# A fused attention, mixer and gated-feed-forward kernel: one weight slice loaded earlier, spreads placed behind given tiles, and four products moved from GpSimd to VectorE

## The chip, the cores and the metric

The kernel runs on one core of a Trainium2 chip. The metric is the device time of one execution in microseconds (us). The engines are PE (TensorE: matmuls, accumulating in PSUM), DVE (VectorE), ACT (ScalarE), POOL (GpSimd) and SP (SyncE, which issues every DMA here). Each engine works through its own instructions in a fixed order and waits on semaphores for the others.

## The reference

Three parts follow one another, in float32 (q, k, v of 2 x 12 x 448 x 64; the token axis is 448, the model axis 768):

```python
# 1 causal attention
scores = where(mask, -1e9, q @ k.T / sqrt(64)); attn = softmax(scores); x = attn @ v     # x: [2, 448, 768]
# 2 mixer: tokens, then channels
u = x + (relu(x.T @ w_tok1) @ w_tok2).T                  # 448 -> 256 -> 448
x = u + relu(u @ w_ch1) @ w_ch2                          # 768 -> 1536 -> 768
# 3 gated feed-forward
h = gelu_tanh(x @ w_in); u, v = h[..., :512], h[..., 512:]
v_n = (v - mean(v)) / sqrt(var(v) + 1e-6) * g_ln
gated = u * (w_sg @ v_n + b_sg[:, None])                 # w_sg mixes the 448 tokens
out = x + gated @ w_out                                  # 512 -> 768
```

The weights are given in float64 and are unpacked on the chip.

## The kernel before, in words

**Numbers.** Matmuls with full precision are made of three f16 (or fp32r) matmuls: a value is split into a high and a low part, and high by high, high by low and low by high are added in PSUM (`mm3`, lines 174 to 181; its three matmuls are L178, L179 and L180 in every trace row). Before an f16 split a tensor is scaled by its largest absolute value. That maximum is found per partition on an engine and then carried over all partitions by `spread` (lines 156 to 161): one small PE matmul of 128x128 (L158) into a PSUM bank, then three small DVE operations (L159 maximum, L160, L161 reciprocal). The split is ACT (high part) and DVE (low part) in `split16` (L165, L166), or ACT, ACT and POOL in `split16p` (L170, L171, L172).

**Weights.** `decode` (lines 104 to 124) loads a float64 slice by DMA into one of two `wraw` buffers, and makes float32 of it with one ACT operation (L120) and two DVE operations (L123, L124). `load_w2` (lines 546 to 555) decodes one of the six slices of w_ch2, in two halves, into buffers `w2m`, of which there are four, and takes the sum of absolute values of each half on ACT (L553) and their maximum on DVE (L151, the column `w2am0` to `w2am5`). `end_w2` (lines 557 to 569) spreads that column and splits the slice. `begin16` and `end16` (lines 599 to 606 and 664 to 672) do the same for the slices of w_in and w_out; w_out has six slices, 4 to 9 of the counter j.

**Stages.** First attention with the token mixing (to about 165 us). Then r: `channel_up`, twelve tiles of 36 matmuls for each of the two batches, u by w_ch1. Then y: `channel_down`, twelve tiles of 36 matmuls, r by w_ch2, written y(m,b) below for slice m and batch b. The loop of lines 608 to 624 makes y(0,0); y(1,0), y(0,1); y(2,0), y(1,1); and so on, and in each round calls `end_w2(m + 2)` and `load_w2(m + 3)`. Each y tile is taken from PSUM by DVE (L233, `yt`), completed by POOL (L235) and its maximum taken by DVE (L146, `yam`). r of batch 1 is split in `split_r(1)` while y(1,0) runs: twelve ACT operations (L165) and twelve on DVE (L166). Then v (`v_ps`) and u (`ug_ps`) of the gated part with the normalisation, then the mixing over tokens (lines 747 to 765): four tiles g of 11 matmuls for each batch (`g_ps`). DVE scales a g tile and adds b_sg (L761, `gt`), POOL multiplies it into the array `ug` (L763; batch 1 in two pieces, since its tokens lie rotated by 64), and DVE takes the maximum (L146, `gtam`). Once the four tiles of a batch are done, their maximum (L151, `gtam16_0`, `gtam16_1`) is spread, and the products are split (`gate16`, `gt_hi` and `gt_lo`). Last come twelve output tiles o of 12 matmuls, and the writing of the result.

**Order.** A scheduler with a timeline simulation of its own sets the order of each engine's instructions when the program is built; the order in which the code is written and the construct `tc.issue_after(x)` (not before instruction x) only guide it. So PE can stand at a spread whose column is late while matmuls that are ready are queued behind it.

Of the kernel before, what the change touches and what calls it, by code (L numbers as in the profile page):

```python
# [28 lines left out]
def mixer_kernel(  # L29
# [18 lines left out]
    nc = tc.nc  # L48
    B, H2, D2, S = q.shape
# [6 lines left out]
    NCC = C // P  # L56
# [117 lines left out]
    def mm3(ps, pairs, begun=False):  # L174

        n, done = len(pairs), []
        for i, ((lh, ll), (rh, rl)) in enumerate(pairs):
            nc.tensor.matmul(ps, lh, rh, start=i == 0 and not begun, stop=False)  # L178
            nc.tensor.matmul(ps, lh, rl, start=False, stop=False)  # L179
            done.append(nc.tensor.matmul(ps, ll, rh, start=False, stop=i == n - 1).ins)  # L180
        return done
# [345 lines left out]
    with rs:  # L527
        ps_d = ctx.enter_context(tc.tile_pool(name="ps_d", bufs=8, space=PSUM, reuse_waits="tile"))
        r1pool = rs.enter_context(tc.tile_pool(name="r1pool", bufs=1, reuse_waits="tile"))
        tmp = rs.enter_context(tc.tile_pool(name="tmp", bufs=3, reuse_waits="tile"))  # L530
        def pst(name):
            return ps_d.tile([P, 512], F32, tag="d", name=name)

        def split_r(b):

            am = top_of(rsum[:, b], f"ram{b}")
            spread(pst("rs_ps"), am, *rsc[b], TOP)
            for c in range(NFF):
                if b == 0:
                    t = r1pool.tile([P, 2, S], F16, name=f"r16_{c}")  # L540
                else:
                    t = (rpool if c < NF0 else r1pool).tile([P, 2, S], F16, tag=f"r{c}_0", name=f"r16_{c}")
                split16(t[:, 0], t[:, 1], r_of[c, b], rsc[b][1][:, 0:1])
                r_of[c, b] = t

        def load_w2(m):

            ms = []
            for i in range(2):
                w = tmp.tile([P, WC], F32, tag="w2m", name="w2m", bufs=4)  # L550
                decode(w, w_ch2[m, :, i * NCC:(i + 1) * NCC, :].rearrange("p a f -> p (a f)"))
                unused = tmp.tile([P, WC], BF16, tag="w2a", name="w2a", bufs=1)
                nc.scalar.activation(unused, w, AF.Abs, accum_out=w2sum[:, m, i:i + 1])  # L553
                ms.append(w)
            w2_begun[m] = ms, top_of(w2sum[:, m], f"w2am{m}")

        def end_w2(m):

            ms, am = w2_begun.pop(m)
            done = spread(pst("w2_ps"), am, *w2sc[m], TOP)  # L560
            ws[m] = []
            for i, w in enumerate(ms):
                if m < 2:
                    t = tmp.tile([P, 2, NCC, P], F16, name=f"w2_{m}{i}", bufs=1)
                else:
                    t = wpool.tile([P, 2, NCC, P], F16, tag=("whi", "wlo")[i], name="w2", bufs=3)
                split16p(*(t[:, h].rearrange("p a f -> p (a f)") for h in range(2)), w, w2sc[m][1][:, 0:1])
                ws[m] += [(t[:, 0, c, :], t[:, 1, c, :]) for c in range(NCC)]
            return done

        w2_begun, ws, w16, begun = {}, {}, {}, []
        tail = 4
        for m in [*range(NF0 - tail), *range(NF0, NFF), *range(NF0 - tail, NF0)]:
            channel_up(m, [1] if m < NF0 else [0, 1], r1pool, ps_d)
            if m == NF0 + 1:
                with tc.issue_after(last_load[0]):
                    load_w2(0)
            if m == NFF - 2:
                end_w2(0)
                load_w2(1)  # L580
            if m == NF0 - tail:
                end_w2(1)
                split_r(0)
            if m == NF0 - 1:
                load_w2(2)

        def to16(b):

            spread(pst("ys_ps"), yam16[b], *ysc[b], TOP)
            nc.vector.tensor_mul(vinv[:, 2 * b:2 * b + 1], ysc[b][0], wvsc[0])  # L590
            hs = slice(64 * b, 64 * b + 64)
            nc.vector.tensor_copy(vinv[hs, 1:2], vinv[hs, 2 * b:2 * b + 1])
            for m in range(NCC):
                y16[m][b] = upool.tile([P, 2, S], F16, tag=f"ul{m}_{b}", name=f"y16_{m}_{b}")
                split16(y16[m][b][:, 0], y16[m][b][:, 1], y32[m][b], ysc[b][1][:, 0:1])
                ts = slice((1 - b) * (S - 64), (1 - b) * (S - 64) + 64)
                nc.vector.tensor_copy(y3[:, :, m, 64 * b:64 * b + 64], y16[m][b][:, :, ts])

        def begin16(src, j):

            k = src.shape[1]
            m = wpool.tile([P, WC], F32, tag="wm", name="wm", bufs=3)[:, :k * P]
            decode(m, src.rearrange("p a f -> p (a f)"))
            am = wams[:, j:j + 1]
            absmax(am, m)
            begun.append((j, k, m, am))

        for m in range(NCC):
            channel_down(m, ws[m], [0], ps_d, tmp)
            if m == 0:  # L610
                with tc.issue_after(mms[0, 0][NFF // 2]):
                    split_r(1)
            if 0 < m < NCC - 1:
                channel_down(m - 1, ws[m - 1], [1], ps_d, tmp)
            if m + 2 < NCC:
                spread_last = end_w2(m + 2)
            with tc.issue_after(spread_last):
                if m + 3 < NCC:
                    load_w2(m + 3)
                for c in ([m], [m], [m], [m], [m, m + 1], [])[m]:  # L620
                    decode(wv32[:, c, :], w_inv[:, c, :])
                    absmax(wvam[:, c:c + 1], wv32[:, c, :])
                if m == NCC - 2:
                    wvam16 = top_of(wvam, "wvam16")
        spread(pst("wv_ps"), wvam16, *wvsc, TOP)
        for c in range(NCC):
            split16(wvh[:, c, :], wvl[:, c, :], wv32[:, c, :], wvsc[1][:, 0:1])
        with tc.issue_after(spread_last):
            for m in range(3):
                begin16(w_inu[m], m)  # L630
        channel_down(NCC - 2, ws[NCC - 2], [1], ps_d, tmp)
        to16(0)
        channel_down(NCC - 1, ws[NCC - 1], [1], ps_d, tmp)
        last_y = last_top[0]
# [8 lines left out]
    z_hi = gp.tile([P, NV, DH], F16, name="z_hi")  # L643
    z_lo = gp.tile([P, NV, DH], F16, name="z_lo")
# [19 lines left out]
    def end16():  # L664

        j, k, m, am = begun.pop(0)
        split = split16 if j < NDC else split16p
        spread(pst("w_ps"), am, winv[:, j:j + 1], wsc[:, j:j + 1], TOP)
        hi = gp.tile([P, k, P], F16, name=f"wh{j}")
        lo = gp.tile([P, k, P], F16, name=f"wl{j}")  # L670
        split(hi.rearrange("p a f -> p (a f)"), lo.rearrange("p a f -> p (a f)"), m, wsc[:, j:j + 1])
        w16[j] = hi, lo
# [66 lines left out]
    def gate16(b):  # L739

        us = slice(b * S, (b + 1) * S)
        spread(pst("gt_ps"), gtam16[b], *gtsc[b], TOP)
        nc.vector.tensor_scalar(oinv[:, b], winv[:, NDC:], gtsc[b][0][:, 0:1], None, ALU.mult)
        for m in range(NDC):
            split16(gt_hi[:, m, us], gt_lo[:, m, us], ug[:, m, us], gtsc[b][1][:, 0:1])

    for b in range(B):
        us = slice(b * S, (b + 1) * S)
        for m in range(NDC):
            if b == 0 and m < 2:  # L750
                end16()
            if b == 1 and m == 2:
                gate16(0)
            ds_ = slice(m * P, (m + 1) * P)
            pg = pst("g_ps")
            nc.tensor.matmul(pg[:, :S], zz[b][:, ds_], sgh[:, 3, :], start=True, stop=False)
            nc.tensor.matmul(pg[:, :S], zz[b][:, ds_], sgl[:, 3, :], start=False, stop=False)
            vts_ = [c + 4 * b for c in range(3)]
            mm3(pg[:, :S], [((z_hi[:, vt, ds_], z_lo[:, vt, ds_]), (sgh[:, c, :], sgl[:, c, :])) for c, vt in enumerate(vts_)], True)
            gt = gw.tile([P, S], F32, tag="gt", name="gt")  # L760
            nc.vector.scalar_tensor_tensor(gt, pg[:, :S], gcol[:, m:m + 1], bb, ALU.mult, ALU.add)  # L761
            for cs, ts in rotated(b):
                nc.gpsimd.tensor_mul(ug[:, m, cs], gt[:, ts], ug[:, m, cs])  # L763
            absmax(gtam[:, b, m:m + 1], ug[:, m, us])
        gtam16[b] = top_of(gtam[:, b], f"gtam16_{b}")
    last_gt = last_top[0]
# [65 lines left out]
```

## Time and profile before

| | |
|---|---|
| time, median of 3 runs | 422.99 us (421.78 to 426.54) |
| the profiled execution | 422.21 us |
| its span, first to last instruction | 420.1 us |
| PE busy | 389.7 us (93%) |
| DVE, ACT, POOL busy | 281.4, 248.5, 207.2 us |
| mean granted clock of PE | 0.994 |

The profiled execution lies between the fastest run and the median; 2.1 us of it lie outside the span. Busy time of PE is made of records whose ends are modelled, so the spacing of matmul starts says more: in y, g and o it is 0.19 us per matmul of 448 columns when nothing is missing. A granted clock of 1.00 is the higher of the two levels of PE (2.4 GHz), 0.50 the lower (1.2 GHz).

### The profile page before, as it was taken

How to read it: one execution, taken by the hardware profiler on the slowest of the kernel's cores; microseconds unless marked ns; L12 is line 12 of the kernel's file. 1: busy time of each engine (PE TensorE's matmuls, PEld its weight loads, DVE VectorE, ACT ScalarE, POOL GpSimd, SP SyncE). 2: the span in 40 equal slices, each digit the busy share in tenths (PEclk: the TensorE clock that was granted, in tenths of full speed). 3: DMA queues.
4: the chain of work that ended last, by engine and by line, in shares of the span. 5: the costliest groups of instructions: out<-in, count | busy, mean ns of one | idle time of the engine just before them, and what ended most of it. 6: DMA issues, size and time to landing. Idle time of an engine off the chain costs nothing.

```text
span 420.1 us, 7291 instructions
## 1 busy us (share of the span) xinstructions
PE 389.7 (93%) x2610; PEld 264.0 (63%) x2610; DVE 281.4 (67%) x689; ACT 248.5 (59%) x481; POOL 207.2 (49%) x211
## 2 busy tenths in 40 slices
PE   5868898796898999999999979999999999999996
PEld 3546777674787999999887534555554445544553
DVE  5979775799935635434356698666896896648832
ACT  3989776589775555754679676543256475562200
POOL 2786847679777573431452255344212666138200
PEclk9999999999999999999999998999999999999999
DMA  7999898999955844765540034436603032100122
GB/s 214 207 283 249 189 143 181 242 290 301 199 139 128 181 145 153 222 230 191 184 135 17 17 110 137 158 131 201 222 0 89 0 101 100 52 1 0 67 109 87
DMA packets 61459, 60.99 MB, mean 145 GB/s; under 512 B 47856, under 2 KB 53104, under 8 KB 61424
## 3 DMA queue, kind: packets, MB, share of 16 engines
q1 hardware_dynamic: 61424, 60.54, 53.3%
q8 instruction: 20, 0.33, 0.3%
q14 instruction: 15, 0.12, 0.1%
HBM read 46.50 MB, written 2.75 MB: 117 GB/s over the span
## 4 chain that ended last, share of the span: by engine, by line
PE 47%; DVE 13%; DMA 12%; POOL 11%; issue 8%; ACT 6%; SPq 2%; POOLq 0%; ACTq 0%; DVEq 0%
PE r_ps L179 6%; PE r_ps L180 6%; PE r_ps L178 6%; PE y_ps L178 5%; PE y_ps L180 5%; PE y_ps L179 5%; DMA vr<-in 5%; DMA pT<-hl 5%; POOL hl L357 3%; PE o_ps L179 2%; PE o_ps L180 2%; PE o_ps L178 2%; DMA wraw<-in 2%; DVE wm L124 2%; POOL wl L172 2%
## 5 line engine op out<-in xcount | busy, mean ns | idle before, releaser
L357 POOL TENSOR_TENSOR hl<-pe,hl 128x512 f16<-128x512 f32 x43 | 54.0, 1264 | 24.3 <-ACT hl L356 23.8
L330 PE MATMUL s_ps<-k,q 128*128 128x64 f32 (+3 forms) x216 | 54.7, 393 | 11.5 <-DVE mx L335 4.8
L100 POOL TENSOR_TENSOR wlo<-wm,whi 128x768 fp32r<-128x768 f32 x19 | 37.6, 1977 | 42.1 <-ACT whi L133 42.0
L178 PE MATMUL r_ps<-uh,whi 128*128 128x448 f32 x144 | 53.6, 372 | 0.0
L179 PE MATMUL r_ps<-ul,whi 128*128 128x448 f32 x144 | 53.3, 370 | 0.0
L180 PE MATMUL r_ps<-uh,wlo 128*128 128x448 f32 x144 | 53.0, 368 | 0.0
L120 ACT ACTIVATE wm<-wraw 128x768 f32<-128x768 f32 (+2 forms) x35 | 28.0, 800 | 41.7 <-DMA wraw<-in 25.9
L178 PE MATMUL y_ps<-r,w 128*128 128x448 f16 x144 | 51.4, 357 | 0.0
L179 PE MATMUL y_ps<-r,w 128*128 128x448 f16 x144 | 51.2, 356 | 0.0
L180 PE MATMUL y_ps<-r,w 128*128 128x448 f16 x144 | 51.2, 356 | 0.0
L123 DVE TENSOR_SCALAR wm<-wm 128x768 int32<-128x768 int32 (+2 forms) x35 | 21.7, 621 | 42.5 <-ACT wm L120 42.5
L330 PEld LDWEIGHTS s_ps<-k,q 128*128 128x128 f32 x216 | 30.2, 198 | 21.7 <-DVE mx L335 5.7
L235 POOL TENSOR_TENSOR y<-yt,ul 128x448 f32<-128x448 f32 x12 | 15.5, 1290 | 48.4 <-DVE yt L233 45.5
L335 DVE CUSTOM_DVE_ANT_0 pe<-s_ps,mask 128x192 f32<-128x192 f32 (+3 forms) x84 | 34.9, 443 | 5.4 <-PE s_ps L330 5.4
L124 DVE SCALAR_TENSOR_TENSOR wm<-wraw,wm 128x768 int32<-128x768 int32 (+2 forms) x35 | 35.4, 1013 | 0.6
L344 ACT ACTIVATE pe<-pe,bias 128x448 f32<-128x448 f32 (+3 forms) x74 | 35.3, 525 | 0.3
L381 PE MATMUL x_ps<-vh,pT 128*128 128x65 f16 (+1 forms) x240 | 25.9, 197 | 6.6 <-DMA pT<-hl 5.9
L356 ACT CAST hl<-pe 128x512 f16<-128x512 f32 x43 | 26.1, 610 | 9.2 <-DMA pT<-hl 8.9
L381 PEld LDWEIGHTS <-pT 128*128 128x128 f16 (+1 forms) x240 | 21.1, 98 | 13.4 <-DMA pT<-hl 8.7
L172 POOL TENSOR_TENSOR w<-w2m,w 128x768 f16<-128x768 f32 x12 | 21.3, 1791 | 15.3 <-ACT w L171 12.6
L179 PEld LDWEIGHTS r_ps<-ul,whi 128*128 128x128 f32 x144 | 27.0, 188 | 2.8 <-issue 0.4
L180 PEld LDWEIGHTS r_ps<-uh,wlo 128*128 128x128 f32 x144 | 27.0, 188 | 2.7 <-issue 0.2
(205 smaller groups left out, 1016.1 us busy)
## 6 DMA issues: line engine op xcount, KB each, us to landing
wraw<-in SPq DMA_DIRECT2D x35, 768.0 KB, 4.3
wraw<-in SPq DMA_DIRECT2D x14, 512.0 KB, 3.7
vr<-in SPq DMA_DIRECT2D x12, 320.0 KB, 3.7
k<-in SPq DMA_DIRECT2D x12, 224.0 KB, 3.1
q<-in SPq DMA_DIRECT2D x24, 112.0 KB, 3.6
out<-ob SPq DMA_DIRECT2D x12, 224.0 KB, 1.9
wraw<-in SPq DMA_DIRECT2D x3, 256.0 KB, 3.1
pT<-hl SPq DMA_TRANSPOSE x43, 4.1
```

The source lines that it names most:

```text
L100: nc.gpsimd.tensor_sub(lo, src, f32(hi))
L120: nc.scalar.activation(m, words.bitcast(F32)[:, :, 1], AF.Prelu, scale=2.0 ** -112, alpha=-(2.0 ** 32))
L124: nc.vector.scalar_tensor_tensor(mi, words[:, :, 0], 29, mi, ALU.logical_shift_right, ALU.bitwise_or)
L172: nc.gpsimd.tensor_sub(lo, m, hi)
L178: nc.tensor.matmul(ps, lh, rh, start=i == 0 and not begun, stop=False)
L179: nc.tensor.matmul(ps, lh, rl, start=False, stop=False)
L180: done.append(nc.tensor.matmul(ps, ll, rh, start=False, stop=i == n - 1).ins)
L330: nc.tensor.matmul(ps[:, o:o + m], qp[:, q0:q0 + P], k2[:, ks], start=True, stop=True)
L335: nc.vector.tensor_tensor_reduce(out=pe[:, cs], in0=ps[:, cs], in1=mask0 if i == 0 else mask[:, MASKS[i]], scale=-1.0 / math.sqrt(D), scal ...
L344: nc.scalar.activation(pe[:, cs], pe[:, cs], AF.Exp, bias=bias[:, j:j + 1], scale=-1.0)
L357: nc.gpsimd.tensor_sub(hl[:, 1], pe, hl[:, 0])
L381: nc.tensor.matmul(o, ph, vh[:, c, h, :D + 1], start=j == 0, stop=False)
```

## The change

Four edits in three places. The fourth slice of w_ch2, `load_w2(3)`, is called right behind `load_w2(2)` at the end of r, and the loop of y loads slice m + 4 in place of m + 3. The `end16` of w_out's slices j = 8 and 9 is called ahead of g tiles 2 and 3 of batch 0, each told not to start before the last matmul of the tile ahead of it, in place of ahead of tiles 0 and 1 with no condition; `gate16(0)` gets the same condition. And the four products of batch 0 are VectorE's.

```diff
@@ the loop over channel_up
             if m == NF0 - 1:
                 load_w2(2)
+                load_w2(3)
@@ the loop over channel_down
             with tc.issue_after(spread_last):
-                if m + 3 < NCC:
-                    load_w2(m + 3)
+                if m + 4 < NCC:
+                    load_w2(m + 4)
@@ the mixing tiles
         for m in range(NDC):
-            if b == 0 and m < 2:
-                end16()
+            if b == 0 and m > 1:
+                with tc.issue_after(gmm[-1]):
+                    end16()
             if b == 1 and m == 2:
-                gate16(0)
+                with tc.issue_after(gmm[-1]):
+                    gate16(0)
...
-            mm3(pg[:, :S], [...], True)
+            gmm = mm3(pg[:, :S], [...], True)
...
             for cs, ts in rotated(b):
-                nc.gpsimd.tensor_mul(ug[:, m, cs], gt[:, ts], ug[:, m, cs])
+                (nc.vector if b == 0 else nc.gpsimd).tensor_mul(ug[:, m, cs], gt[:, ts], ug[:, m, cs])
```

Lines of the changed kernel behind 586 lie one to three further down (L761 there is L764, L763 is L766).

What this makes of the order on the engines is seen at three places. The first is DVE at the end of r, from the maximum of r (`ram1`) on; `yt` is the taking of y(0,0), `rinv1` and `rs1` are the scale of r in batch 1, `w2m` the halves of slice 3 and `w2am3` its column. Before:

```order
L151 TENSOR_REDUCE ram1_3272<-rsum_70 128x1
L233 SCALAR_TENSOR_TENSOR yt_3267<-y_ps_3229,yinv_2583,uh0_0_94 128x448
L159 TENSOR_REDUCE rinv1_2586<-rs_ps_3274 128x1
...
L123 TENSOR_SCALAR w2m_3328<-w2m_3328 128x768
L123 TENSOR_SCALAR w2m_3336<-w2m_3336 128x768
...
L146 TENSOR_REDUCE yam_2601<-y0_0_3269 128x1
L124 SCALAR_TENSOR_TENSOR w2m_3328<-wraw_3329,w2m_3328 128x768
L166 SCALAR_TENSOR_TENSOR r16_0_3279<-r_2658,rs1_2587,r16_0_3279 128x448
L124 SCALAR_TENSOR_TENSOR w2m_3336<-wraw_3337,w2m_3336 128x768
```

Now:

```order
L151 TENSOR_REDUCE ram1_3290<-rsum_70 128x1
L123 TENSOR_SCALAR w2m_3229<-w2m_3229 128x768
L124 SCALAR_TENSOR_TENSOR w2m_3229<-wraw_3230,w2m_3229 128x768
L123 TENSOR_SCALAR w2m_3237<-w2m_3237 128x768
L124 SCALAR_TENSOR_TENSOR w2m_3237<-wraw_3238,w2m_3237 128x768
L233 SCALAR_TENSOR_TENSOR yt_3285<-y_ps_3247,yinv_2583,uh0_0_94 128x448
L159 TENSOR_REDUCE rinv1_2586<-rs_ps_3292 128x1
L159 TENSOR_REDUCE w2inv2_2592<-w2_ps_3333 128x1
L151 TENSOR_REDUCE w2am3_3245<-w2sum_2600 128x1
L160 TENSOR_SCALAR rinv1_2586<-rinv1_2586 128x1
```

The four operations that decode slice 3 now stand ahead of the taking of y(0,0), and its column among the small operations behind; before, the column came behind all splits of r and two operations of wv. On ACT the two sums of slice 3 (L553) move in the same way from behind the twelve splits to ahead of them.

The second place is PE at the end of y(0,1) (`y_ps_3413` now). Before, the spread of `w2am3` stood behind the tile's last matmul and ahead of y(2,0). Now it stands behind the 28th of its 36 matmuls, and behind the tile come two matmuls of y(2,0), then eleven of y(1,1) (`y_ps_3536`), then y(2,0) again:

```order
L178 MATMUL y_ps_3413<-r16_9_3324,w2_01_2957 128x448
L158 LDWEIGHTS w2am3_3245
L158 MATMUL w2_ps_3456<-ident_b_79,w2am3_3245 128x128
L179 LDWEIGHTS w2_01_2957
L179 MATMUL y_ps_3413<-r16_9_3324,w2_01_2957 128x448
...
L180 MATMUL y_ps_3413<-r16_11_3330,w2_01_2957 128x448
L178 LDWEIGHTS w2_3338
L178 MATMUL y_ps_3493<-r16_0_3082,w2_3338 128x448
L179 LDWEIGHTS w2_3338
L179 MATMUL y_ps_3493<-r16_0_3082,w2_3338 128x448
L178 LDWEIGHTS w2_10_3067
L178 MATMUL y_ps_3536<-r16_0_3297,w2_10_3067 128x448
```

The third matmul of a slice's pair, L180, is the one that needs the low part of the slice; that of y(2,0) now stands behind the eleven of y(1,1).

The third place is DVE in the mixing of batch 0, from the first `gt` on. Now, with the products (L766) among the rows and one spread's small operations round each of the next two tiles:

```order
L764 SCALAR_TENSOR_TENSOR gt_4619<-g_ps_4607,gcol_4024,bb_4023 128x448
L766 TENSOR_TENSOR ug_4018<-gt_4619,ug_4018 128x448
L146 TENSOR_REDUCE gtam_2613<-ug_4018 128x1
L764 SCALAR_TENSOR_TENSOR gt_4635<-g_ps_4623,gcol_4024,bb_4023 128x448
L159 TENSOR_REDUCE winv_2614<-w_ps_4639 128x1
L766 TENSOR_TENSOR ug_4018<-gt_4635,ug_4018 128x448
L160 TENSOR_SCALAR winv_2614<-winv_2614 128x1
...
L764 SCALAR_TENSOR_TENSOR gt_4705<-g_ps_4693,gcol_4024,bb_4023 128x448
L151 TENSOR_REDUCE gtam16_0_4691<-gtam_2613 128x1
```

The last `gt` shown is that of batch 1's first tile; as before it stands ahead of `gtam16_0`. On PE the spread of slice 8 moves from ahead of g tile 0 to behind tile 1, that of slice 9 from behind tile 0 to behind tile 2; the spreads of `gtam16_0` (behind the second g tile of batch 1) and of `gtam16_1` stay where they were. On POOL the low parts of slices 8 and 9 (L172) now stand right ahead of the products of batch 1.

## Rows read from the trace of the kernel before

**Rows 1.** Waits of PE from 134 us on: engine line, waited for: us, times, longest.

```profile
PE w_ps L158 <- DVE w2am L151: 3.0, 1, 3.0
PE w_ps L158 <- DVE wams L146: 1.0, 1, 1.0
PE gt_ps L158 <- DVE gtam L151: 0.6, 1, 0.6
```

**Rows 2.** Windows: us, busy time (count) by engine, PE's granted clock, DMA share, GB/s.

```profile
248.99:252.00 3.01, 0.01 (x1) 0.02 (x2) 2.25 (x4) 0.65 (x1) 3.01 (x3) 0.87 0.00 0
252.00:254.70 2.70, 2.70 (x9) 1.16 (x10) 2.63 (x6) 1.23 (x3) 2.45 (x2) 0.51 0.59 175
```

**Rows 3.** Timeline of PE, y(0,1) into y(2,0): start, us, what, idle before.

```profile
248.64 0.35 PE L180 MATMUL y_ps<-r,w 128*128 128x448 f16 x1
251.99 0.29 PE L158 MATMUL w_ps<-ident_b,w2am 128*128 128x128 bf16 x1 [3.00 <-DVE w2am L151]
252.06 0.58 PE L178 MATMUL y_ps<-r,w 128*128 128x448 f16 x1
...
254.66 0.35 PE L179 MATMUL y_ps<-r,w 128*128 128x448 f16 x1
```

**Rows 4.** Timeline of DVE, end of r to `w2am3`.

```profile
235.26 0.68 DVE L233 SCALAR_TENSOR_TENSOR yt<-y_ps,yinv,uh 128x448 f32<-128x448 f32 x1 [3.87 <-PE y_ps L180]
...
237.24 1.00 DVE L123 TENSOR_SCALAR w2m<-w2m 128x768 int32<-128x768 int32 x2
...
240.29 0.96 DVE L124 SCALAR_TENSOR_TENSOR w2m<-wraw,w2m 128x768 int32<-128x768 int32 x1
...
246.52 1.87 DVE L166 SCALAR_TENSOR_TENSOR r<-r,rs,r 128x448 f16<-128x448 f32 x3
...
251.79 0.14 DVE L151 TENSOR_REDUCE w2am<-w2sum 128x1 bf16<-128x2 f32 x1
```

**Rows 5.** Timeline of ACT: the second half of slice 3.

```profile
232.42 0.90 ACT L120 ACTIVATE w2m<-wraw 128x768 f32<-128x768 f32 x1 [0.42 <-POOL w L172]
```

**Rows 6.** Timeline of POOL: slice 2's first low part.

```profile
249.69 1.63 POOL L172 TENSOR_TENSOR w<-w2m,w 128x768 f16<-128x768 f32 x1
```

**Rows 7.** Timeline of PE round the spreads of slice 9, `gtam16_0` and `gtam16_1`.

```profile
371.80 0.35 PE L180 MATMUL g_ps<-sgh,z_lo 128*128 128x448 f16 x1
373.19 0.23 PE L158 MATMUL w_ps<-ident_b,wams 128*128 128x128 bf16 x1 [1.04 <-DVE wams L146]
...
383.47 0.35 PE L180 MATMUL g_ps<-sgh,z_lo 128*128 128x448 f16 x1
384.42 0.23 PE L158 MATMUL gt_ps<-ident_b,gtam 128*128 128x128 bf16 x1 [0.60 <-DVE gtam L151]
...
393.00 0.35 PE L180 MATMUL o_ps<-gt_hi,wl 128*128 128x448 f16 x1
393.37 0.23 PE L158 MATMUL gt_ps<-ident_b,gtam 128*128 128x128 bf16 x1
```

**Rows 8.** Timeline of DVE in the mixing of batch 0.

```profile
372.44 0.69 DVE L146 TENSOR_REDUCE wams<-wm 128x1 bf16<-128x512 f32 x1
...
373.83 0.67 DVE L761 SCALAR_TENSOR_TENSOR gt<-g_ps,gcol,bb 128x448 f32<-128x448 f32 x1
...
378.02 0.62 DVE L146 TENSOR_REDUCE gtam<-ug 128x1 f32<-128x448 f32 x1 [1.80 <-POOL ug L763]
```

**Rows 9.** Timeline of POOL: batch 1's first product; then one while DVE splits.

```profile
383.72 1.27 POOL L763 TENSOR_TENSOR ug<-gt,ug 128x64 f32<-128x64 f32 x2 [0.23 <-DVE gt L761]
...
388.28 1.38 POOL L763 TENSOR_TENSOR ug<-gt,ug 128x384 f32<-128x384 f32 x1
```

**Rows 10.** Groups by shape: busy, mean ns. DVE `ul` and POOL `wl`.

```profile
L444 DVE TENSOR_TENSOR ul<-u_ps,uh 128x448 fp32r<-128x448 f32 x12 | 7.4, 620 | 9.2 <-ACT uh L443 9.0
L172 POOL TENSOR_TENSOR wl<-wm,wh 128x512 f16<-128x512 f32 x6 | 7.0, 1170 | 16.5 <-ACT wh L171 16.5
```

**Rows 11.** Timeline of DVE: the splits of `gt_lo`, the first three together.

```profile
387.47 2.67 DVE L166 SCALAR_TENSOR_TENSOR gt_lo<-ug,gts,gt_hi 128x448 f16<-128x448 f32 x3
```

More of the change, by code (lines that the diff above doesn't have):

```diff
@@ L758, in mixer_kernel @@
             vts_ = [c + 4 * b for c in range(3)]
-            mm3(pg[:, :S], [((z_hi[:, vt, ds_], z_lo[:, vt, ds_]), (sgh[:, c, :], sgl[:, c, :])) for c, vt in enumerate(vts_)], True)
+            gmm = mm3(pg[:, :S], [((z_hi[:, vt, ds_], z_lo[:, vt, ds_]), (sgh[:, c, :], sgl[:, c, :])) for c, vt in enumerate(vts_)], True)
             gt = gw.tile([P, S], F32, tag="gt", name="gt")
```

## The prediction

> **What bounds the kernel now.** I read the waits of PE first, then the timeline of PE at the spacing of the matmul starts, then the other engines around each hole, and the built order last. The reader is to see that from 134 us on PE is the bound and has three holes only: it waited 3.0, 1.0 and 0.6 us, each time at a spread, for the column that DVE was to deliver [rows 1]. Nothing else is worth much there: matmuls of 448 columns start every 0.19 us everywhere else in y, g and o. So a change pays if it closes a hole, and costs if it opens one; what it does on DVE, ACT or POOL counts only where PE comes to wait.
>
> The first hole costs more than its wait. y(0,1)'s last matmul starts at 248.64 and the spread of slice 3 at 251.99; with 0.19 due, 3.16 us are lost. Behind it the granted clock is 0.51 of full, the lower level, for the stretch 252.00 to 254.70, after 3.01 us in which PE did next to nothing [rows 2]. Seven matmuls take from 252.06 to 254.66, 2.60 in place of 7 x 0.19 = 1.32, so another 1.28 us go [rows 3]. That is 4.44 us. The other holes by the same count: 371.80 to 373.19 loses 1.20, and 383.47 to 384.42 loses 0.76 [rows 7]; no clock falls there. All three make 6.40 us.
>
> **The change, part by part.**
>
> *Slice 3 of w_ch2 loaded earlier.* The reader is to see in the DVE timeline that slice 3's column was ready only at 251.79 + 0.14, because its decode stood among the splits of r and its column behind them [rows 4]. The load itself was not late: ACT was unpacking the second half at 232.42, held by a buffer that POOL freed, not by a transfer [rows 5]. The built order puts the four DVE operations ahead of the taking of y(0,0). They cost 2 x 0.50 + 2 x 0.96 = 2.9 us, and DVE had stood idle for 3.87 us just there, until 235.26 [rows 4]. The second half is ready at 232.42 + 0.90 = 233.3 and needs 1.46 more, so DVE is through at 234.8: the cover holds with 0.5 us to spare, and without it the delay would land on the splits of r. Those gain: 1.9 us of L124 no longer lies among them (they had ended at 248.39, within half a microsecond of the tile that eats them [rows 3, 4]). The two sums on ACT, by estimate each as long as an unpacking (0.90 [rows 5]), end near 236.6, and the column with them; the spread stands on PE eight matmuls before the end of y(0,1), at about 247.3. The column is over 10 us early, and the hole goes, with the slow clock behind it: **-4.44 us**.
>
> What is late next is slice 2's low part, made by POOL. Its first half ended at 249.69 + 1.63 = 251.3 [rows 6]. In the new order y(0,1) ends at 248.8, and two matmuls of y(2,0) and eleven of y(1,1) come before one that needs it: 13 x 0.19 puts that at 251.3. So even if POOL gains nothing the wait is about nil, and it should gain, since y(1,0) is taken earlier. Slice 4 follows in the same buffers as before and its load is asked for no later; I cost it at nothing, covered by the y tiles between.
>
> *Spreads of slices 8 and 9.* Slice 9's column is ready at 372.44 + 0.69 = 373.1 [rows 8]; its spread now stands two g tiles later on PE (2 x 11 x 0.19 = 4.2 us). The hole closes: **-1.20 us**. The low parts that follow are wanted by output tiles only some 20 us on.
>
> *Batch 0's products on VectorE.* No row shows this operation on DVE. The nearest is the subtraction `ul` of the same 448 columns at 0.62 us [rows 10]; with nothing in its way the product can't be much shorter, and I take 0.62. The other end is a product that waits for a whole POOL operation of 1.17 first [rows 10], 1.79 us. DVE then needs for one tile `gt` 0.67, product 0.62 and `gtam` 0.62 [rows 8, 10], 1.91 us, against 2.08 for the 11 matmuls of a g tile: it keeps up. From 373.13 on: one spread's operations 0.5 (two took 0.70 there: 373.83 less 373.13 [rows 8]), four tiles 7.64, two more spreads 0.7, `gt` of batch 1 0.67, the top 0.14 as for `w2am` [rows 4]: the column of batch 0 at 382.8. Without the holes PE reaches that spread at 384.42 - 1.96 = 382.46 [rows 7]. A wait of 0.35 stays out of 0.76, so this part gives **-0.41 us**. At the upper end, with two of the four products blocked, it is 2.3 us later and the gain of both late holes is gone.
>
> *Batch 1 behind it.* POOL's first product of batch 1 began 0.7 us before the spread of batch 0 [rows 7, 9]. Now `gt` of that tile stands behind DVE's fourth product and maximum, and on POOL slices 8 and 9 come first, so it begins at about the spread. The chain from there to batch 1's column is in order on DVE and POOL and was already 0.18 us late for PE (393.00 to 393.37, with 0.19 due [rows 7]). I charge **+0.70 us**; its ends are 0 and 1.4, twice the shift.
>
> Here rows and page can be weighed. POOL's 1.38 us product at 388.28 lies over DVE's three splits, which took 2.67 us where three splits of the same size took 1.87 for r [rows 4, 9, 11]: an operation of each does not run beside the other. The Trainium skill ("SBUF — State Buffer", section "Who interferes with whom") says that a DVE instruction with two SBUF inputs and a GpSimd instruction that reads SBUF lock each other out for the whole instruction. The trace agrees at this place. By that rule the products on DVE, two SBUF inputs each, can be blocked where `gt`, with one input in PSUM, can not.
>
> *Sum:* -4.44 - 1.20 - 0.41 + 0.70 = **-5.35 us**. Against the profiled execution's own 422.21 that makes 416.9; it lies 0.8 under the median of the runs, which would give 417.6. I take **417.2 us**, span about 415.
>
> **The rivals.**
>
> *The products collide on VectorE.* If POOL's low parts of slices 7, 8 and 9 (1.17 each) fall on the products, the chain of batch 0 is late again. For it: the port rows above, and that slices 7 to 9 are split in just these 8 us. Against: by my sum slice 7's low part ends near the second product's start, and slice 8's and 9's lie either side of the fourth. Two collisions eat 2.3 us; the first hole's 4.44 remains, less up to 0.7: 418 to 419.2. This is the skill's rule come true. Chance 0.17.
>
> *The first wait moves.* PE waits in y(2,0) for POOL's low part, or at y(4,0) for slice 4, whose high parts on ACT now stand behind unpackings of wv that wait for transfers. It decides from the point where POOL's first low part ends after 251.3. A wait of 2 us gives back 2, and over 3 us, as the first hole shows, the slow clock's 1.28 too: 419 to 421.5. For it: the order is built on simulated times. Against: before, with POOL held up, that part was just on time. Chance 0.13.
>
> *Slower: the decode in front of the queue.* DVE works in order, and slice 3 now stands ahead of the taking of y(0,0), the scale of r and its twelve splits. If its halves are late, all of that is. Splits with 2.4 us in hand (1.9 saved and 0.5 before) pass every microsecond beyond on to PE in y(0,1). The gain of 5.35 is eaten when the second half comes 7.8 us later than 232.42, and the kernel is 1% slower, 427.2, at 12 us. For it: it is a real order and nothing else can pass. Against: ACT unpacked at 232.42 without a transfer in its way. Chance 0.03, at 423 to 428.
>
> *It does less than it says.* Since the load was already early, only the order on DVE and ACT is new; if the scheduler's built order had kept the column behind the splits nothing would happen, but it doesn't. What is left is that some of it goes elsewhere: 421.5 to 423. Chance 0.05.
>
> **How the numbers follow.** Forecast 0.62, at 417.2; its own range is 415.4 (all 6.4 us from the fastest run, 421.78) to 418.6 (417.6 with batch 1's charge at its end and some more of the wait). The range for 8 in 10 runs from 415.0, which leaves 0.4 for the scatter between runs, to 420.0, which takes in the collision case and a third of the moved wait. About 1% is what a measurement of this kernel can tell from no change; 1% under 422.99 is 418.8. Faster: nearly all of the forecast (0.60), two thirds of the collisions (0.11), and a little of the moved wait (0.02), 0.73. Slower by over 1%: 0.03. The rest, 0.24, is within 1%.
>
> **What would show it.** In the profile after: no wait of PE at the spread of slice 3 and a granted clock of 1.00 from 245 to 260; slice 3's column on DVE near 236.6; no wait at slice 9's spread; the products on DVE at 0.62, or at 1.2 and more if blocked; a wait of a few tenths at `gtam16_0` and of about 0.9 at `gtam16_1`. I am wrong if PE shows a wait of over 1 us between 249 and 300, if the products' mean is over 1 us, or if the span is above 418.

## The result, and the profile after

The changed kernel took 418.99 us (median of 17 runs, 416.86 to 423.87); the kernel before, beside it, 424.22 us (17 runs, 421.60 to 427.20). The ratio is 0.9879, with a 95% interval of 0.9850 to 0.9908: 1.2% faster, about 5.1 us. The forecast was 417.2 us in a range of 415.0 to 420.0.

The profiled execution of after took 421.92 us with a span of 420.1. It came to the y stage 4 us later than the one of before did (first matmul of y at 232.24 against 228.24). Everything ahead of y is the same program, and in other profiled executions of the changed kernel y began between 230.5 and 234.0. So the two are compared by stage, each from its first matmul to the first of the next stage.

| us | y | v | ug | g | o to its last start | y to o |
|---|---|---|---|---|---|---|
| before | 86.62 | 27.47 | 27.57 | 18.75 | 27.30 | 187.71 |
| after | 82.37 | 29.39 | 27.52 | 16.81 | 27.66 | 183.75 |
| difference | -4.25 | +1.92 | -0.05 | -1.94 | +0.36 | -3.96 |
| forecast | -4.44 | 0 | 0 | -1.61 | +0.70 | -5.35 |

So these stages hold some 4.0 of the 5.1 us. Another 0.3 lies outside the span, which leaves out 2.1 us of each run of the kernel before and 1.8 of each run of the changed one; no run shows why. The last 0.8 or so, ahead of y or behind o, is not located.

Waits of PE from y on in the profile after: engine, line, what it waited for, total, times, longest.

```profile
PE ys_ps L158 <- DVE yam L151: 1.7, 1, 1.7
PE gt_ps L158 <- DVE gtam L151: 0.4, 1, 0.4
```

None of the three waits of before [rows 1] is left. The second line is `gtam16_1`, which the forecast charged. The first is one that neither the forecast nor a rival had.

**The first hole.** PE's timeline of after at the spread of slice 3, DVE's at its column, and the window from 245 to 260 (columns as in [rows 2]).

```profile
251.09 0.35 PE L178 MATMUL y_ps<-r,w 128*128 128x448 f16 x1
251.28 0.22 PE L158 MATMUL w_ps<-ident_b,w2am 128*128 128x128 bf16 x1
```

```profile
240.32 0.16 DVE L151 TENSOR_REDUCE w2am<-w2sum 128x1 bf16<-128x2 f32 x1
```

```profile
245.00:260.00 15.00, 15.00 (x82) 7.79 (x80) 12.35 (x20) 11.75 (x18) 10.90 (x6) 1.00 0.12 36
```

The column stands 10.8 us ahead of its spread, PE is busy for the whole 15 us, and the granted clock is 1.00, the higher level, where it had been 0.51 behind the hole [rows 2, 3].

**The mixing stage.** PE after at the spreads of slice 9, `gtam16_0` and `gtam16_1`; then DVE on the first product, its maximum, and the top of batch 0.

```profile
377.63 0.35 PE L180 MATMUL g_ps<-sgh,z_lo 128*128 128x448 f16 x1
377.81 0.22 PE L158 MATMUL w_ps<-ident_b,wams 128*128 128x128 bf16 x1
...
383.92 0.35 PE L180 MATMUL g_ps<-sgh,z_lo 128*128 128x448 f16 x1
384.11 0.22 PE L158 MATMUL gt_ps<-ident_b,gtam 128*128 128x128 bf16 x1
...
393.41 0.23 PE L158 MATMUL gt_ps<-ident_b,gtam 128*128 128x128 bf16 x1 [0.38 <-DVE gtam L151]
```

```profile
374.66 0.62 DVE L766 TENSOR_TENSOR ug<-gt,ug 128x448 f32<-128x448 f32 x1
375.32 0.62 DVE L146 TENSOR_REDUCE gtam<-ug 128x1 f32<-128x448 f32 x1
...
382.83 0.15 DVE L151 TENSOR_REDUCE gtam<-gtam 128x1 bf16<-128x4 f32 x1
```

The first two spreads follow the matmul before them by 0.18 to 0.19 us, where 1.39 and 0.95 had passed [rows 7]. All four products took 0.62.

**The new wait.** PE after at the spread of `yam16_1` (from batch 1's last y tile), and DVE after from the third slice of w_inu to that column. w_inu is the half of w_in that makes u; wv is the half that makes v, and `wvinv` is its scale, taken from its spread.

```profile
318.27 0.38 PE L180 MATMUL v_ps<-wvh,y 128*128 128x512 f16 x1
320.40 0.23 PE L158 MATMUL ys_ps<-ident_b,yam 128*128 128x128 bf16 x1 [1.74 <-DVE yam L151]
```

```profile
301.12 0.98 DVE L123 TENSOR_SCALAR wm<-wm 128x768 int32<-128x768 int32 x1 [0.65 <-ACT wm L120]
...
304.99 0.28 DVE L159 TENSOR_REDUCE wvinv<-wv_ps 128x1 f32<-128x128 f32 x1
...
317.62 0.67 DVE L233 SCALAR_TENSOR_TENSOR yt<-y_ps,yinv,uh 128x448 f32<-128x448 f32 x1
...
320.18 0.16 DVE L151 TENSOR_REDUCE yam<-yam 128x1 bf16<-128x6 f32 x1
```

And the same of before, DVE first, then PE.

```profile
302.77 0.28 DVE L159 TENSOR_REDUCE wvinv<-wv_ps 128x1 f32<-128x128 f32 x1
...
317.95 0.16 DVE L151 TENSOR_REDUCE yam<-yam 128x1 bf16<-128x6 f32 x1
```

```profile
318.74 0.22 PE L158 MATMUL ys_ps<-ident_b,yam 128*128 128x128 bf16 x1
```

Here the lost 1.9 us are read. PE starts v 4.25 us earlier than before, counted from the start of y (82.37 against 86.62). DVE makes `wvinv` only 1.78 earlier by the same count (304.99 - 232.24 = 72.75; before 302.77 - 228.24 = 74.53). From there to `yam16_1` it takes 15.19 us after and 15.18 before. In before the column was ready at 318.11, 0.63 ahead of PE. 4.25 - 1.78 - 0.63 = 1.84: what PE now has to wait (1.74 by the row; 2.13 between the two starts where 0.22 is due).

### The profile page after: what moved, and what is told of

It reads as the page before. It is cut to its first block, busy times and chain, and to the rows that moved or that the text cites. A ratio compares the mean times of both kernels' runs of the same rounds, so it can differ in the third digit from the quotient of the medians.

```text
span 420.1 us, 7290 instructions
## 1 busy us (share of the span) xinstructions
PE 392.3 (93%) x2610; PEld 267.7 (64%) x2610; DVE 283.2 (67%) x693; ACT 249.0 (59%) x481; POOL 202.8 (48%) x207
## 4 chain that ended last, share of the span: by engine, by line
PE 41%; DMA 17%; DVE 13%; POOL 11%; ACT 10%; issue 6%; SPq 2%; POOLq 0%; ACTq 0%
DMA wraw<-in 8%; DMA pT<-hl 6%; PE r_ps L179 5%; PE r_ps L180 5%; PE r_ps L178 5%; POOL hl L357 4%; ACT r L165 3%; DMA vr<-in 3%; PE ug_ps L179 2%; PE ug_ps L180 2%; PE ug_ps L178 2%; PE v_ps L180 2%; PE v_ps L178 2%; PE v_ps L179 2%; PE o_ps L179 2%
## 5 line engine op out<-in xcount | busy, mean ns | idle before, releaser
L330 PE MATMUL s_ps<-k,q 128*128 128x64 f32 (+3 forms) x216 | 57.9, 413 | 10.0 <-DMA q<-in 4.8
L180 PE MATMUL r_ps<-uh,wlo 128*128 128x448 f32 x144 | 53.0, 368 | 0.0
L178 PE MATMUL y_ps<-r,w 128*128 128x448 f16 x144 | 50.8, 353 | 0.0
L179 PE MATMUL y_ps<-r,w 128*128 128x448 f16 x144 | 50.7, 352 | 0.0
L180 PE MATMUL y_ps<-r,w 128*128 128x448 f16 x144 | 50.6, 352 | 0.0
L330 PEld LDWEIGHTS s_ps<-k,q 128*128 128x128 f32 x216 | 32.7, 211 | 21.2 <-DVE mx L335 5.1
L180 PEld LDWEIGHTS r_ps<-uh,wlo 128*128 128x128 f32 x144 | 27.0, 188 | 2.7 <-issue 0.2
L178 PEld LDWEIGHTS r_ps<-uh,whi 128*128 128x128 f32 x144 | 27.1, 188 | 2.6 <-issue 0.2
```

Of the source, the lines that this page charges most:

```text
L330: nc.tensor.matmul(ps[:, o:o + m], qp[:, q0:q0 + P], k2[:, ks], start=True, stop=True)
```

## The experiments

Theory 1 was that the wait comes from the new order on DVE, in which the decode of wv's column 1 stands ahead of yt(1,1). Theory 2: it belonged to the one late execution. The first four runs (again, load, mix, wv_late) shared a chip.

**again**, the changed kernel unchanged:

> The changed kernel once more, unchanged. Theory 1 (the new wait comes from the order on VectorE, in which the decode of wv's column 1 now stands ahead of yt(1,1) and waits for its transfer): TensorE waits at the spread of yam16_1 again, 1 to 2 us, in this execution too, and wvinv is made some 4 us after TensorE's spread of it; 418.5 to 419.5 us, about 5 less than before. Theory 2 (the wait belonged to the one execution profiled, whose early stages ran 4 us late): no wait at that spread, the stage between y and ug is back at 27.5 us.

418.60 us, ratio 0.9871 (0.9820 to 0.9923). The wait is there with 1.7 us, also in two further executions, **after_c** and **after_d**, the marks for later runs. Theory 2 falls: after_d began y at 230.5, and wv_late below at 228.3, as early as before did, and both have the same wait. The stretch from y to o took 183.6, 184.0 and 184.4 us in the three, so differences below 1 us between single executions are not read in it. The scatter is in y (82.20, 82.61, 83.05), where after_c and after_d also wait 0.3 and 0.8 us at batch 0's spread, `yam16_0`; g and o repeat within 0.02.

> The changed kernel on the same chip, as the mark for the kernel above: the wait of 1.7 us at the spread of yam16_1, 183.4 to 183.6 us from the start of y to the end of o, ratio to before 0.987.

> The changed kernel on the same chip, as the mark for the kernel above: 183.4 to 183.6 us from the start of y to the end of o, ratio to before 0.988.

They came to 0.9881 (0.9825 to 0.9937) and 0.9880 (0.9849 to 0.9911).

**load**, the slice's load alone:

```diff
             if m == NF0 - 1:
                 load_w2(2)
+                load_w2(3)
...
-                if m + 3 < NCC:
-                    load_w2(m + 3)
+                if m + 4 < NCC:
+                    load_w2(m + 4)
```

> Only the slice's load is moved; the spreads and the products of the mixing stage are as before. Theory 1: the y stage gives 4.2 us, the wait at the spread of yam16_1 takes 1.9 back, so 2.3 us less than before (ratio 0.994 to 0.995), with the wait in its trace. Theory 2: 4.2 less (0.990), no such wait. The hole at slice 9's spread (1.2) and the wait at gtam16_0 (0.76) stand as before under both.

420.09 us, ratio 0.9918 (0.9885 to 0.9952). Waits of PE from y on:

```profile
PE ys_ps L158 <- DVE yam L151: 1.8, 1, 1.8
PE gt_ps L158 <- DVE gtam L151: 0.5, 1, 0.5
```

The load alone brings the new wait (1.8): it is this edit that moves it there. But 3.9 us remain by stages (y 82.1, v 29.4, g 17.4, o 27.3; y to o 183.85), more than the 2.3 expected, since the hole at slice 9's spread is gone too, without any edit there. Its column is ready 1.90 us after the start of g (3.23 in before), and PE comes to the spread at 2.08.

**mix**, the spreads and products alone:

```diff
-            if b == 0 and m < 2:
-                end16()
+            if b == 0 and m > 1:
+                with tc.issue_after(gmm[-1]):
+                    end16()
...
-                nc.gpsimd.tensor_mul(ug[:, m, cs], gt[:, ts], ug[:, m, cs])
+                (nc.vector if b == 0 else nc.gpsimd).tensor_mul(ug[:, m, cs], gt[:, ts], ug[:, m, cs])
```

(`gate16(0)` likewise.)

> Only the spreads and products of the mixing stage are changed; the slice's load is as before. Both theories: 1.6 us less than before (1.9 in the mixing stage, 0.4 given back at gtam16_1; ratio 0.996), the hole at slice 3's spread stays at 3 us with the clock low behind it, and TensorE does not wait at the spread of yam16_1.

422.46 us, ratio 0.9978 (0.9942 to 1.0014). Its trace has the wait of 3.0 at slice 3 and none at `yam16_1`; g took 16.8 and o 27.8, together 1.4 less than before. The size agrees, though the runs alone don't tell it from nothing. In g and o together before took 46.05 us, the load alone 44.74, mix 44.61 and after 44.47: with the first edit in, the second has only 0.3 left to close. The times of the runs don't show this: again came out 0.9871 on the chip where load came out 0.9918, some 2 us apart with intervals that overlap. Of these, 0.3 lies outside the span, where load has 2.1 as before and again 1.8; the rest is not located.

**wv_late**, theory 1's repair:

```diff
-                for c in ([m], [m], [m], [m], [m, m + 1], [])[m]:
+                for c in ([m], [], [m - 1], [m - 1, m], [m, m + 1], [])[m]:
```

> The change, and the decodes of wv's columns 1 to 3 one chunk later, so that column 1's stands behind spread 4 on VectorE and no longer ahead of yt(1,1). Theory 1: yt(1,1) is taken within 1 us of TensorE's end, wv3's buffer comes free earlier, the wait at the spread of yam16_1 goes: 1.9 us less than the change, about 417 us, ratio to before 0.983 to 0.985. Theory 2: as the change, 0.988, in whatever execution. A third reading (a transfer of wm2 that is late by itself and stands ahead of wvinv on VectorE) also expects the wait to stay: 0.988, or worse where the later decodes keep the buffers longer.

419.66 us, ratio 0.9895 (0.9855 to 0.9935). Wait of PE at these spreads:

```profile
PE ys_ps L158 <- DVE yam L151: 2.7, 2, 1.7
```

The 1.7 stays. Batch 0's spread waits 0.9 here, little more than the 0.8 of after_d, so that is not put down to this edit. Theory 1 falls. What stays the same is the stretch from `wvinv` to `yam16_1`: 15.18 to 15.20 us in before, the executions of after, load, mix and wv_late, and in every kernel that follows. So theory 3: behind `wvinv` DVE is full but for two waits for POOL's sums (0.66 and 1.25), and what holds `wvinv` back is the last wait in front of it, at the decode of w_inu's third slice (0.65 us of waiting for its unpacking and 2.5 of work).

**wm2_v** takes that decode into the v stage:

```diff
-            for m in range(3):
+            for m in range(2):
                 begin16(w_inu[m], m)
...
+        if vt == 2:
+            with tc.issue_after(last_v):
+                begin16(w_inu[2], 2)
```

> The change, and the decode and column maximum of the third slice of w_inu taken out of the end of the y stage into the v stage, behind the statistics of its second tile. Theory 3 (the runs so far: VectorE works without a gap for 15.2 us from wvinv to yam16_1, and wvinv stands behind this slice's decode, 0.72 us of waiting for its transfer and 2.5 us of work): wvinv is made within 0.5 us of TensorE's spread of it, TensorE does not wait at the spread of yam16_1, the v stage takes 27.5 us again, and as the late spreads keep slice 9's hole closed, all of it stays: 1.7 to 1.9 us less than the change, about 417 us, ratio to before 0.983. Rival, theory 4 (the end of batch 1 is late for another reason, the sum on GpSimd or the low parts of batch 0 behind which yt(5,1) stands): the wait stays at 1 us or more, 0.987.

419.59 us, ratio 0.9908 (0.9872 to 0.9945). PE at the spread of `yam16_1` and at that of w_inu's fourth slice:

```profile
316.27 0.38 PE L180 MATMUL v_ps<-wvh,y 128*128 128x512 f16 x1
316.49 0.22 PE L158 MATMUL ys_ps<-ident_b,yam 128*128 128x128 bf16 x1
...
335.92 0.38 PE L180 MATMUL v_ps<-wvh,y 128*128 128x512 f16 x1
337.82 0.23 PE L158 MATMUL w_ps<-ident_b,wams 128*128 128x128 bf16 x1 [1.52 <-DVE wams L146]
```

The cause holds: the wait at `yam16_1` is gone. `wvinv` is still made 2.2 us behind PE's spread of it (301.06 against 298.87), not within the 0.5 expected, but that is early enough. The forecast of the time does not hold: the column of the next slice is late instead (1.52), v still takes 29.2 us, and y to o 183.5.

**load_wm2v**, the same with the mixing stage as before:

> The load moved and the third slice of w_inu decoded in the v stage, mixing stage as before. Theory 3, with the reading that the load alone closed the hole at slice 9's spread because TensorE reached it 1.9 us later: no wait at yam16_1's spread (1.9 less than the load alone), but the hole at slice 9's spread is there again with about 1 us, and the wait at gtam16_0 of 0.5 to 0.8: 4.2 to 4.5 less than before (ratio 0.990), some 1.6 us longer than the kernel with the late spreads as well. If slice 9's column came earlier for a reason of its own, its hole stays closed: 5.4 less, 0.987.

420.02 us, ratio 0.9913 (0.9872 to 0.9955). Waits of PE from y on:

```profile
PE w_ps L158 <- DVE wams L146: 2.3, 2, 1.1
PE gt_ps L158 <- DVE gtam L151: 0.6, 1, 0.6
PE ys_ps L158 <- DVE yam L151: 0.2, 1, 0.2
```

One of the two waits on `wams` is the fourth slice's (1.11), the other slice 9's: that hole is back as soon as `yam16_1` no longer delays PE. g takes 18.9 where the load alone had 17.4, and y to o is 2.7 less than before, not the 4.2 to 4.5 expected, as v keeps the fourth slice's wait.

**noprod**, after with the products on POOL:

```diff
-                (nc.vector if b == 0 else nc.gpsimd).tensor_mul(ug[:, m, cs], gt[:, ts], ug[:, m, cs])
+                nc.gpsimd.tensor_mul(ug[:, m, cs], gt[:, ts], ug[:, m, cs])
```

> The change with the first batch's products on GpSimd as before (load and late spreads kept). The forecast's pricing: the product waits for weight unpackings on GpSimd (1.17 us each) and takes 1.2 instead of 0.6, so gtam16_0 is late by the wait of before, 0.76, and by up to the 1.2 that the closed hole gives TensorE: 0.4 to 1.6 us longer than the change. If the products do not bound it: the change's time, no wait at gtam16_0. The wait at yam16_1 stays at 1.7 in both.

421.19 us, ratio 0.9954 (0.9924 to 0.9985). By stages g takes 17.1 and o 28.3, together 1.0 more than after. Wait of PE there:

```profile
PE gt_ps L158 <- DVE gtam L151: 1.0, 1, 1.0
```

It is `gtam16_1`, not `gtam16_0` as expected: POOL is late for batch 1, whose first product it begins 13.05 us after the start of g, in after 11.48. The runs show some 3 us (0.9954 against 0.9880, on different chips). The stages explain 1.0 of it and the time outside the span 0.3 (2.1 here, 1.8 in after); I can't say where the rest is. Beside load, which has neither the late spreads nor the products, noprod takes 0.7 more in g and o (45.4 against 44.7): once the load is moved, the late spreads alone cost time, and the products on DVE bring it back.

**wm2_w** also queues the fourth slice's spread behind the v tiles:

```diff
-        if vt > 2:
+        if 2 < vt < NV - 1:
             end16()
...
+    with tc.issue_after(vmm[-1]):
+        end16()
```

> As the kernel before it with the third slice of w_inu decoded in the v stage, and the spread of the fourth slice's column, where TensorE then waited 1.5 us, queued behind the last of the v tiles. Theory 3: no wait at the spread of yam16_1 and none at this one, the v stage takes 27.4 to 27.6 us as before the change (29.2 to 29.4 in the runs with a wait), and 1.7 to 1.9 us less than the change from the start of the y stage to the end of o: 181.7 to 181.9 us there against 183.4 to 183.6; ratio to before 0.983. If it is not more than a wait that moves along, the gain is taken at the next column again (slice 9's or gtam16_0), and that stretch stays above 183.

420.79 us, ratio 0.9928 (0.9890 to 0.9965). v takes 27.5 us, as expected. But y to o takes 184.4 where 181.7 to 181.9 were expected: the wait has moved again, and g takes 19.4. PE at `gtam16_0`, then DVE at slice 9's decode and the first `gt`:

```profile
382.36 0.23 PE L158 MATMUL gt_ps<-ident_b,gtam 128*128 128x128 bf16 x1 [2.40 <-DVE gtam L151]
```

```profile
371.32 0.43 DVE L123 TENSOR_SCALAR wm<-wm 128x512 int32<-128x512 int32 x1 [3.38 <-ACT wm L120]
...
373.69 0.67 DVE L769 SCALAR_TENSOR_TENSOR gt<-g_ps,gcol,bb 128x448 f32<-128x448 f32 x1
```

PE had begun its second g tile at 369.3, so the first lay ready over 4 us while DVE stood 3.38 us in front of slice 9's decode.

**w9_c** puts that decode behind the second column of batch 0:

```diff
-    begin16(w_out[NDC + 1], NDC + NDC + 1)
...
-            if b == 0 and m > 1:
+            if (b, m) in ((0, 2), (1, 1)):
                 with tc.issue_after(gmm[-1]):
                     end16()
...
+            if (b, m) == (0, 1):
+                with tc.issue_after(col):
+                    begin16(w_out[NDC + 1], NDC + NDC + 1)
```

> The kernel before it (third slice of w_inu in the v stage, the fourth's spread behind the v tiles), and slice 9's decode taken from ahead of the first batch's mixing on VectorE to behind its second column, its spread two mixing tiles later. Theory 5 (what is left is an order on VectorE: in the kernel before it gt(0) was read 4.2 us after TensorE had it, since slice 9's decode stands ahead and waits 3.4 us for its unpacking): gt(0) is read within 0.5 us of TensorE's end, the wait of 2.4 at gtam16_0 shrinks to 0.5 or less, 181.8 to 182.4 us from the start of the y stage to the end of o against 183.4 to 183.6 in the change, ratio to before 0.982 to 0.985. Rival (the mixing stage is bound by VectorE's work itself, or the wait moves to slice 9's spread or gtam16_1): 183 or more, ratio as the change's.

418.63 us, ratio 0.9867 (0.9831 to 0.9904), with after_d at 0.9880 beside it. DVE on the first `gt` and the first two products, and POOL in between:

```profile
371.60 0.68 DVE L768 SCALAR_TENSOR_TENSOR gt<-g_ps,gcol,bb 128x448 f32<-128x448 f32 x1 [1.41 <-PE g_ps L180]
372.31 0.62 DVE L770 TENSOR_TENSOR ug<-gt,ug 128x448 f32<-128x448 f32 x1
...
374.48 1.58 DVE L770 TENSOR_TENSOR ug<-gt,ug 128x448 f32<-128x448 f32 x1
```

```profile
374.42 1.16 POOL L172 TENSOR_TENSOR wl<-wm,wh 128x512 f16<-128x512 f32 x1 [2.56 <-ACT wh L171]
```

`gt` is read as soon as PE has it, the wait at `gtam16_0` falls from 2.40 to 0.58, and g from 19.4 to 17.6. The stretch from y to o took 183.3, on the rival's side (183 or more), where 181.8 to 182.4 were expected, since in this execution `yam16_1` kept PE 0.7 us, g still had 0.8 more than after, and o 0.3 more than before. Against after_d's 184.4 it is 1.1 less, and the intervals of the two ratios overlap widely: no version was shown to beat the changed kernel.

## Why the prediction was right, and where it was not

- **First hole, -4.44:** right in mechanism and size. -4.25 in the profiled pair, y 82.2 to 83.05 in four executions against 86.6, wait and slow clock both gone. The column came at 240.32, which is 8.1 after the start of y where the forecast's 236.6 was 8.4.
- **The step that failed is that -4.44 was booked whole, with nothing given back later in y.** Behind the hole the prediction looked at slice 2's low part and at slice 4 ("I cost it at nothing, covered by the y tiles between"). Slice 4 did cost nothing: PE in after has no wait from 249 to 318. But I asked what PE meets next up to 251 us and took all that DVE does from there to the end of y as ahead of PE. It was ahead by 0.63 us at `yam16_1`; PE gained 4.25 and DVE 1.78. That is worth +1.9 (v 29.4 against 27.5), seen in all four executions of the change and in load. Rival 2 had the kind (the first wait moves, a wait of 2 gives back 2), but at y(2,0) and y(4,0) instead, for POOL's low part or slice 4.
- **Slice 9's spread, -1.20:** closed in after, and by mix also without the first edit. In after it would have closed by itself, so the terms may not be added: in g and o the load alone gives -1.31, mix -1.44, both together -1.58.
- **Products, -0.41:** right in the price, 0.62 each as taken from `ul` [rows 10], and no collision. Counted from the start of g, PE reached `gtam16_0` after 12.6 us, as forecast; the column was ready after 11.5 and not 12.9, so not even the wait of 0.35 remained. Two things made it early. The sum for DVE was too long: mix and wm2_v, without a wait at `yam16_1`, have the column at 12.4 and 12.5. The rest, 1.0, is what DVE had gained on PE through that wait. noprod puts the products' worth at 1.0 by stages.
- **`gtam16_1`, +0.70:** +0.36, between its ends.
- **The range and chances:** 418.99 lies in 415.0 to 420.0, and the measured gain of 5.1 us is close to the sum's 5.35. In part that is luck: from y to o the four executions gained 3.3 to 4.1 us, and the sum had no term for the 0.3 outside the span or for the rest. That 418.99 is 1.8 over 417.2, the size of the missed wait, is chance too, since the kernel before took 424.22 beside it and not the 422.99 that the forecast started from. Of my signs for being wrong the span came true (420.1, 4 us of it the late start of y in this execution); the wait of over 1 us came at 318, past the 249 to 300 that I had named.

Why DVE gained only 1.78 us can be read in part. Its waits from the start of y to `wvinv`, before and then after:

```profile
DVE yt L233 <- PE y_ps L180: 8.5, 3, 3.9
DVE wv L123 <- ACT wv L120: 3.2, 3, 2.3
DVE wm L123 <- ACT wm L120: 1.8, 2, 1.1
DVE w2m L123 <- ACT w2m L120: 0.7, 1, 0.7
```

```profile
DVE wv L123 <- ACT wv L120: 5.3, 4, 2.3
DVE w2m L123 <- ACT w2m L120: 4.7, 4, 1.9
DVE wm L123 <- ACT wm L120: 1.9, 2, 1.3
```

Before, DVE waited 8.5 us for PE's tiles and 5.7 for unpackings of weights; after, it waits for no tile, 11.9 for unpackings, and for POOL's sums 3.9 where it had been 1.6. The last four of these started on ACT within 0.04 us of a landing, and each transfer was issued within 0.1 us of DVE emptying one of the two raw buffers (for w_inu's third slice emptied 296.04, issued 296.10, landed 300.16). So DVE seems to be paced there mainly by the round trip of two buffers and not by PE. That is a reading of the traces: no run changed the number of buffers, and whether a third would pay stays open.

## What to carry to other kernels

A hole closed on the busiest engine is paid out only as far as every later meeting point has slack: list for each later wait how far ahead the other engine is (here 0.63 us at `yam16_1`), and take the least, before the gain is booked. Holes of one engine pair need not add: here a wait that delayed PE covered the hole behind it, which came back when the wait was closed. With work in order on one queue, read which operation stands in front of the gapless stretch that ends at the late column: moving it moves the wait, to the next column, so count the chain to the end of the program.

## What the runs showed of the hardware

A product on DVE took 0.62 us alone and 1.58 where it met POOL's subtraction of 1.16 (374.48 against 374.42 in w9_c): 0.96 longer, most of the 1.10 that POOL still had to run. `gt`, which reads one operand from PSUM and took 0.67 alone [rows 8], took 0.69 at 375.88 in after beside the same kind of subtraction, at 375.53:

```profile
375.53 1.16 POOL L172 TENSOR_TENSOR wl<-wm,wh 128x512 f16<-128x512 f32 x1 [4.69 <-ACT wh L171]
```

```profile
375.88 0.69 DVE L764 SCALAR_TENSOR_TENSOR gt<-g_ps,gcol,bb 128x448 f32<-128x448 f32 x1
```

The rule of the Trainium skill that the prediction named ("SBUF — State Buffer", "Who interferes with whom") agrees with both. The collision rival's price of 1.17 for each was near the 0.96 measured; its condition did not come about, as the four products of batch 0 met no operation of POOL in after, mix, wm2_v or wm2_w and took 0.61 to 0.63 in each.
